# A searched table takes the place of a rehearsed schedule, and the clamp of the norm moves to VectorE

## The chip, the core and the metric

The kernel runs on one core of one Trainium2 chip. The metric is the device time of one execution in microseconds (us). The engines have short names in the profile: PE is TensorE (PEld its weight loads), DVE is VectorE, ACT is ScalarE, POOL is GpSimd, SP is the engine that issues most DMAs. [...]

## The reference

An attention block with inducing points feeds a SwiGLU feed-forward block. There are B = 4 batches of N = 12416 rows of C = 128 numbers, m = 32 inducing rows, and a hidden width of 1536.

```python
def mab(q, kv):
    s = scale * (q @ kv.transpose(0, 2, 1))
    s = s - s.max(-1, keepdims=True)
    a = np.exp(s)
    a /= a.sum(-1, keepdims=True) + 1e-09
    return a @ kv
h = mab(I, x)                 # 32 inducing rows look at all rows of the batch
x = mab(x, h)                 # every row looks at the 32 results
...
rms = np.sqrt(np.mean(x * x, axis=-1, keepdims=True) + 1e-06)
xn = x / rms * rms_g
g = xn @ w_gate
silu = g * (1.0 / (1.0 + np.exp(-g)))
val = xn @ w_val
return silu * val @ w_out
```

All is float32. The second attention's weights have only 32 numbers a row, so the kernel never forms the attention's output: it multiplies h into the gate and value weights once for each batch (the stacks `sg` and `sv`) and applies them to the 32 weights of each row. The norm needs only a 32 x 32 matrix of products of h (`gram`) and those weights. The clamp of the diff stands in that norm: the mean square is held at 1e-6 or more before the power -1/2.

## The kernel before, in words

**Slots.** A batch is cut into 7 sets of rows, and these into 25 units: 20 of 512 columns, 4 of 480 and one of 256. A unit has 12 slots, one for each block of 128 hidden numbers. There are 300 slots for each batch and 1200 in all. A slot is written by `slot` in `ffn`: the gate product (L723, one pass of PE into a PSUM bank `gv`), SiLU on ScalarE (L731; in a few slots tanh at L727 with two more VectorE operations), the value product (L734), their product on VectorE (L740), and then the steps of other work that are due.

**Three kinds of block.** The output product of a block (`u` times a block of `w_out`) can be done in two ways.
- A plain block writes the product to a buffer `u` in SBUF, and PE takes it in float32 at L660 (two records each in the trace, `acc<-u,wo`).
- A three-pass block is split into parts of fewer bits, and PE takes three faster passes: L681 and L683 into the bank `u3`, L660 into `acc` (`project3`). The kind "sums" leaves the product in its PSUM bank (L740, `gv<-silu,gv`), takes the high part on ScalarE (L705), the rest on VectorE (L706) and the difference of both on POOL (L715). The kind "differences" writes `u`, and needs two ScalarE copies (L709, L714) and two POOL operations (L710, L715). The parts lie in rings of buffers (`idle` holds the free ones).

A string of letters gives each slot its kind: `s`, `d`, or `.` for plain. The strings before have three parts of 300; the second serves batches 1 and 2.

**Order of products.** Products are not done in the slot that makes their operand, but some slots later, first in, first out in two lists (`plain` and `kara`). Before the gate product a slot calls `products(0)`, before the value product `products(1)`, and before the n-th step of other work `products(n + 2)`. What each call does is in `picks`. Before the change, `rehearse` fills `picks`: a model in Python with fixed costs for each step (`COST`) that walks through all slots as the engines would, and whenever PE would stand idle takes a product that is ready, or up to two when more than a reserve of seven are waiting.

**Banks and buffers.** The products of gate and value and most attention steps share five PSUM banks `gv0` to `gv4`. The rehearsal also gives the banks: always the one that comes free first. `u` has nine buffers, `work` three, both taken in turn.

**Other work in the slots.** While the slots of batch b run, the first attention of batch b + 1 is done in steps that `schedule(b)` puts at fixed slots: `turn_x` (VectorE transposes of loaded columns), `scores1`, `max1` to `max3`, `exp1_of`, `turn_e`, `sum_h`, `fold_l`, `divide`, `turn_h`, `square_h`, `stack`, `place` (DMAs that put pieces of the new stacks in place), `scores2`, `row_max`, `sub_max`, `exp2`. For each set of rows there is a seam, which scales its attention weights by the norm: `turn_a`, `square` (L507), `turn_z` (L513, L514), `scale` (L518), `root` (two POOL operations, L523 the clamp and L524 the power), `apply` (L528), `turn_b` (L532), `split` (L538, L541). Then `gather`, a DMA of the split halves, brings each unit's operand `a` ten slots before the unit starts. The loop at the end of the kernel calls, in each slot, the steps that are due now (`waiting`), then those of the plan. After the last slot all remaining products are done, plain ones first, and then what is still in `waiting`.

Of the kernel before, what the change touches and what calls it, by code (L numbers as in the profile page):

```python
# [18 lines left out]
P = 128  # L19
R = 4  # L20
# [3 lines left out]
def kernel(  # L24
# [87 lines left out]
    work = pool("work", 3)  # L112
# [4 lines left out]
    up = pool("up", HELD)  # L117
# [46 lines left out]
    nc.gpsimd.memset(mhalf[:], -0.5)  # L164

# [9 lines left out]
    sel = up.tile([P, 512], F32R, name="u")[:, 0:2 * P].rearrange("p (k r c) -> p k r c", k=2, r=R)  # L175
# [39 lines left out]
    def rounding(i, c):  # L215
# [20 lines left out]
        def power():  # L236
# [12 lines left out]
            e = st["e"] = work.tile([P, 512], I32, name="we", tag="work")  # L249
# [38 lines left out]
    BANKS5, turn, turns = 5, [0], []  # L288

    def bank():  # L290
        if turns:
            n = turns.pop(0)
        else:
            n = turn[0] % BANKS5
            turn[0] += 1
        return ps_gv.tile([P, 512], F32, name="gv", tag=f"gv{n}")

    def attention(b, load_next):
# [42 lines left out]
        def max2():  # L341
            ps = bank()
            nc.tensor.transpose(ps[0:1, 0:P], st["mx"][:], ident[:])
            row = once.tile([1, m], F32, name="row")
            nc.vector.reduce_max(out=row[:], in_=ps[0:1, 0:P].rearrange("p (q m) -> p m q", m=m), axis=AX.X)
            row4 = st["row4"] = once.tile([1, R, m], F32, name="row4")
            nc.vector.tensor_scalar_mul(out=row4[:], in0=row[:].unsqueeze(1).to_broadcast((1, R, m)), scalar1=-SCALE)

        def max3():
            ps = bank()  # L350
            nc.tensor.matmul(ps[:, 0:1], st["row4"][:].rearrange("p q m -> p (q m)"), ones[0:1, 0:1],
                             start=True, stop=True)
            nbias = st["nbias"] = small.tile([P, 1], F32, name="nbias")
            nc.vector.tensor_copy(out=nbias, in_=ps[:, 0:1])

        def exp1_of(s0, s1):
# [8 lines left out]
            if s1 == NS:  # L365
                nc.vector.reduce_sum(out=st["hl"][:, C:C + 1], in_=st["ls"][:, 0:k + 1], axis=AX.X)

        def turn_e(s):
            e = st["e", s] = (once.tile([P, P], F32, name="hT") if b and per[s] < R else
                              work.tile([P, per[s] * m], F32, name="e", tag="work") if b else  # L370
                              up.tile([P, 512], F32, name="u"))[:, 0:per[s] * m]
# [20 lines left out]
        def fold_l():  # L392

            ps = bank()
# [61 lines left out]
        def stack(i):  # L456
# [5 lines left out]
            hi, lo = st["halves", i] = [work.tile([P, 512], F32R, name=n, tag="work") for n in ("whi", "wlo")]  # L462
# [28 lines left out]
    def seam(b, s):  # L491
# [9 lines left out]
        def turn_a():  # L501
            eT = st["eT"] = work.tile([P, 512], F32, name="eT", tag="work")
# [6 lines left out]
        def turn_z():  # L509
            ps = st["ps"]  # L510
            z = st["z"] = work.tile([P, n, m], F32, name="z", tag="work")
# [4 lines left out]
        def scale():  # L516
            ms = numbers("ms")
            nc.vector.reduce_sum(out=ms, in_=st["z"][rows, :, :], axis=AX.X)  # L518
            st["ms"] = ms

        def root():
            rs = st["rs"] = numbers("rs")
            nc.gpsimd.tensor_scalar(out=rs, in0=st["ms"], scalar1=1e-6, scalar2=None, op0=ALU.max)  # L523
            nc.gpsimd.tensor_tensor(out=rs, in0=rs, in1=mhalf[rows, 0:n], op=ALU.pow)  # L524
# [5 lines left out]
        def turn_b():  # L530
            aT = st["aT"] = work.tile([P, 512], F32, name="aT", tag="work")
# [38 lines left out]
    def soon(k, step):  # L570

        waiting.append([k, step])

# [73 lines left out]
    def ffn(b, u):  # L647
# [72 lines left out]
        def slot(j, products, steps, tanh):  # L720
# [14 lines left out]
            t = v if kinds.get((b, u, j)) == "sums" else up.tile([P, 512], F32, name="u")  # L735
# [109 lines left out]
    if B > 1:  # L845
        for _ in range(R):
            load_channels(*pieces[1].pop(0))

    COST = {"turn_x": (0, .63), "scores1": (1.07, .7), "max1": (0, .1), "max2": (.23, .85), "max3": (.2, .1), "turn_e": (0, .63),
            "exp1_of": (0, 0, 1.14), "sum_h": (2.0, .25), "fold_l": (.16, .15), "divide": (0, .6), "turn_h": (.3, .8),  # L850
            "square_h": (.2, .76), "stack": (1.3, 1.32), "scores2": (1.19, .63), "row_max": (0, .59), "sub_max": (0, 0, 0, 1.01),
            "exp2": (0, 0, 1.0), "turn_a": (0, .63), "square": (1.02,), "turn_z": (0, 1.23), "scale": (0, .6),
            "root": (0, 0, 0, 2.9), "apply": (0, 0, 0, 1.01), "turn_b": (0, .63), "split": (0, 0, .51, 1.25),
            "power": (0, .45), "power_number": (0, 0, .63), "upper": (0, .6), "upper_number": (0, 0, .53), "sign": (0, .6),
            "lower": (0, .6, 0, 1.26), "stack_of": (.87, 0, .5), "stack_low": (0, .62), "split_wo": (0, 0, .7, 1.52), "split_last": (0, 0, .35, .65)}
    BANKS = {"scores1", "sum_h", "max2", "max3", "fold_l", "turn_h", "square_h", "stack", "scores2", "square", "stack_of"}
    AFTER = {"max2": "max1", "max3": "max2", "fold_l": "exp1_of", "turn_h": "divide", "square_h": "turn_h", "square": "turn_a",
             "sum_h": "turn_e", "scores1": "turn_x", "stack": "turn_h", "root": "scale", "apply": "root"}
    ENGINES = ("PE", "DVE", "ACT", "POOL")
    TAIL = {"PE": .17, "DVE": .09, "ACT": .11, "POOL": .04}  # L860
# [96 lines left out]
    def near(b, k, first, last):  # L957
        return any(e + first <= k < e + last for e in plans[b][1])

    def given(b, k, u, j):  # L960
        return plans[b][0].get(k, []) + seams.get((b, u, j), [])

    kinds, picks = {}, {}
    letters = """
        ..........................dd...dsd...d....dssd..dssdss.ssd..sdd.sdd.dd...ss.ssd.ss...dsdsdd.s...sssd
        sdd..s..sdsssd.dsd..dsdd..dd.s......s..ddd..dssssssssd..dssssd.ssd..s.d.ssssss..ssssssssdd..ss.dddss
        sd..dsssssd.ss..s.sdss.sds..ssssssssds..s.ssdssd.d..s...d.d..s..s.s.sdsssd...ss.ss.s.s..ssdssssddd..
        ..ssdd..sd..sd.ssdds.d...sds.s.s.s...dssdsd.sd..dsssd.ss.d..ssdssdd.s...ssdd..sdsd...ssssddsds...sss
        .ssdsd..sds.sds.dd..dsssd..d.d.....ss.ds.d..sssssdsssd..sdsssdss.s..sdds.ss.ss..ssssssdsdd...sdssssd
        sd..d.sssdds.s..ssss.ssssd..s.ssssdssd..ssss.sdssd.....sd.d.....s.sssd.s.s...sssd.ssss..ssssssssds..  # L970
        .s....dss..ssdsssd.sss..sd..s.d.sssss.sssds..sdssssss.s.ss.sssdsssd...s.sss..sd.sssss.sss.dsdssdss.s
        ss.ss.sssss.sds.ssd..ss.sds..sd.ssssd..ssssss..ssds.sssss.ssssd..s.ssss..sds.sssssssssd..ssssssss.ds
        ..sssssss.dsds.s..ssss.ds.sssdds...ssss.ssssssdsss..sdsssd...s..sss.s..dsssdd.ds...dsssssssd.sd.dd..
    """
    letters = "".join(letters.split())
    BLOCKS = [letters[NU * NJ * n:NU * NJ * (n + 1)] for n in (0, 1, 1, 2)]

    def rehearse():

        at = dict.fromkeys(ENGINES, 0.0)  # L980
        free, open_banks = [0.0] * 5, {}
        taken, done = [0.0] * SILU, {}
        rounded = {weight[one]["lower"]: one for one in chunks}
        queues, uses, later, left = {"plain": [], "three": []}, [0], [], {}
        split = {"u3": 0.0, "all": 0}
        idle, leaving = list(range(RING)), []

        def run(e, us, *after):
            at[e] = max([at[e]] + [one + 0.04 for one in after]) + us
            return at[e] + TAIL[e]  # L990

        def bank():
            n = free.index(min(free))
            turns.append((n + turn[0]) % BANKS5)
            return n

        def soon(k, step):
            later.append([k, step])

        def bank_of(unit):  # L1000
            older = flat.index(unit) - 2
            if older < 0 or flat[older] not in left:
                return 0.0
            return left[flat[older]].get("turned", 1e9)

        def has(kind, by):
            if not queues[kind]:
                return False
            t, unit = queues[kind][0][:2]
            if left[unit]["left"] == NJ:  # L1010
                t = max(t, bank_of(unit))
            if kind == "three" and not left[unit]["three"]:
                t = max(t, split["u3"])
            return t <= by

        def ready():
            return sum(one[0] <= at["PE"] for q in queues.values() for one in q)

        def issue(kind, to):
            to.append(kind)  # L1020
            t, unit, w, n = queues[kind].pop(0)
            split["all"] -= 1
            st = left[unit]
            if st["left"] == NJ:
                t = max(t, bank_of(unit))
                assert t < 1e9
            if kind == "plain":
                end = run("PE", 0.858 * w, t)
            else:
                end = run("PE", 0.697 * w, t)  # L1030
                give_back(n, idle, leaving)
                st["three"] += 1
                st["open"] -= 1
                st["end"] = end
                copy(st, w)
            st["left"] -= 1
            st["end"] = end
# [200 lines left out]
```

## Time and profile before

| | us |
|---|---|
| median of 3 runs (lowest, highest) | 1615.83 (1615.65, 1616.07) |
| the profiled execution | 1615.95 |
| its span, first to last instruction | 1614.0 |
| PE matmul busy | 1593.5 (99%) |
| DVE busy | 1438.5 (89%) |
| POOL busy | 1434.7 (89%) |
| ACT busy | 1307.4 (81%) |
| PE weight loads busy | 1100.1 (68%) |

The first slot's gate product starts at 54.5 us; the batches' first gate products are at 54.5, 461.1, 852.5 and 1245.2 us. DMA takes a small share (70 GB/s on average). In the groups of the page each line gives source line, engine, operation, tiles, shapes, count, then busy time and the mean length of one in ns, then the idle time of the engine just before and who ended it. In a timeline the columns are the start, the length, the engine, the line and the operation, and in brackets the idle time before it with what ended it. Matmuls overlap, so that the step from one start to the next tells what one costs.

### The profile page before, as it was taken

Reading aid. Unit: us, or ns where it says so; the run is one execution under the profiler, and the core shown is the slowest. Engines: PE = TensorE matmul, PEld = TensorE weight load, DVE = VectorE, ACT = ScalarE, POOL = GpSimd, SP = SyncE. Lnnn points to the kernel's source line nnn. Section 1 sums busy time; section 2 is a strip of 40 time slices with the busy share of each in tenths; the row PEclk is TensorE's granted clock in tenths of the full one; section 3 lists DMA queues with packets and bytes.
Section 4 is the critical chain, followed back from the end, with each engine's and each line's share of the span. In section 5 each row is a group of like instructions: output and inputs, shape, how many; then the busy total and the mean of one; then the engine's idle time right before and its main releaser. Section 6 shows DMA issues by size and latency. Waiting matters only on the chain.

```text
span 1614.0 us, 26024 instructions
## 1 busy us (share of the span) xinstructions
PE 1593.5 (99%) x7169; PEld 1100.1 (68%) x7169; DVE 1438.5 (89%) x2471; ACT 1307.4 (81%) x2461; POOL 1434.7 (89%) x1182
## 2 busy tenths in 40 slices
PE   8999999999999999999999999999999999999998
PEld 6546667756676666776677666676667677777776
DVE  4879988999889997999888999799989999999996
ACT  4678888877887888887888888888788888888886
POOL 1379999999899999999888999899988899999997
PEclk9999999999999999999999999999999999999999
DMA  7455524443462241624344323262221212212111
GB/s 263 92 74 85 104 52 89 94 97 60 72 97 50 44 95 27 134 64 96 65 68 79 62 42 82 49 139 69 57 38 30 39 30 40 40 27 44 36 37 28
DMA packets 389186, 112.57 MB, mean 70 GB/s; under 512 B 365072, under 2 KB 369712, under 8 KB 386480
## 3 DMA queue, kind: packets, MB, share of 16 engines
q1 hardware_dynamic: 388304, 110.82, 34.9%
q8 instruction: 57, 0.93, 0.3%
q14 instruction: 89, 0.73, 0.2%
q10 hardware_dynamic: 736, 0.08, 0.0%
HBM read 53.95 MB, written 27.00 MB: 50 GB/s over the span
## 4 chain that ended last, share of the span: by engine, by line
PE 83%; POOL 5%; ACT 3%; issue 2%; DVE 1%; SPq 1%; DMA 0%; POOLq 0%; DVEq 0%; ACTq 0%
PE acc L660 28%; PE gv L723 16%; PE gv L734 15%; PE u L683 10%; PE u L681 10%; PE gv L330 2%; POOL xn L715 2%; POOL rs L524 1%; PE gv L386 1%; POOL xn L710 1%; PE gv L507 1%; ACT silu L731 1%; SPq L470 0%; ACT sc L447 0%; ACT xn L705 0%
## 5 line engine op out<-in xcount | busy, mean ns | idle before, releaser
L731 ACT ACTIVATE silu<-gv 128x512 f32<-128x512 f32 (+2 forms) x1186 | 688.8, 587 | 166.0 <-PE gv L723 150.2
L715 POOL TENSOR_TENSOR xn<-xn,xn 128x512 fp32r<-128x512 f32 (+2 forms) x605 | 745.7, 1252 | 70.2 <-DVE xn L706 30.2
L734 PE MATMUL gv<-a,sv 128*128 128x512 f32 (+2 forms) x1188 | 603.3, 508 | 1.3 <-DVE u L740 0.6
L723 PE MATMUL gv<-a,sg 128*128 128x512 f32 (+2 forms) x1188 | 486.3, 410 | 4.6 <-ACT silu L731 2.2
L740 DVE TENSOR_TENSOR u<-silu,gv 128x512 f32<-128x512 f32 (+2 forms) x633 | 414.9, 661 | 68.6 <-PE gv L734 35.5
L660 PE MATMUL acc<-u,wo 128*128 128x512 f32 (+2 forms) x822 | 410.7, 583 | 0.6 <-DVE u L740 0.6
L740 DVE TENSOR_TENSOR gv<-silu,gv 128x512 f32<-128x512 f32 (+2 forms) x553 | 367.7, 668 | 44.1 <-PE gv L734 31.5
L723 PEld LDWEIGHTS gv<-a,sg 128*128 128x128 f32 x1188 | 223.8, 188 | 171.8 <-ACT silu L731 37.2
L734 PEld LDWEIGHTS gv<-a,sv 128*128 128x128 f32 x1188 | 223.8, 188 | 123.4 <-issue 43.1
L705 ACT ACTIVATE xn<-gv 128x512 fp32r<-128x512 f32 (+2 forms) x434 | 253.1, 583 | 58.6 <-DVE gv L740 47.4
L706 DVE SCALAR_TENSOR_TENSOR xn<-xn,gv 128x512 fp32r<-128x512 f32 (+2 forms) x434 | 284.5, 655 | 10.5 <-ACT xn L705 5.8
L681 PE MATMUL u<-xn,xn 128*128 128x512 f32 (+2 forms) x581 | 228.5, 393 | 0.0
L660 PE MATMUL acc<-xn,more 128*128 128x512 f32 (+2 forms) x581 | 226.4, 390 | 1.9 <-POOL xn L715 1.9
L710 POOL TENSOR_TENSOR xn<-u,xn 128x512 fp32r<-128x512 f32 (+2 forms) x171 | 216.1, 1264 | 13.3 <-ACT xn L709 13.3
L660 PEld LDWEIGHTS acc<-u,wo 128*128 128x128 f32 x822 | 154.1, 188 | 36.9 <-issue 5.1
L660 PEld LDWEIGHTS acc<-xn,more 128*128 128x128 f32 x581 | 109.0, 188 | 32.1 <-POOL xn L715 10.3
L681 PEld LDWEIGHTS u<-xn,xn 128*128 128x128 f32 x581 | 109.2, 188 | 25.7 <-issue 5.3
L715 POOL TENSOR_TENSOR sg<-sg 128x512 fp32r<-128x512 f32 (+1 forms) x92 | 118.1, 1283 | 5.5 <-DVE sg L706 1.7
L715 POOL TENSOR_TENSOR sv<-sv 128x512 fp32r<-128x512 f32 (+2 forms) x92 | 118.0, 1282 | 5.4 <-DVE sv L706 2.8
L709 ACT ACTIVATE xn<-u 128x512 fp32r<-128x512 f32 (+2 forms) x171 | 105.5, 617 | 17.6 <-DVE u L740 14.4
L683 PE MATMUL u<-xn,more 128*128 128x512 f32 (+2 forms) x294 | 113.3, 385 | 0.2 <-POOL xn L710 0.2
L683 PE MATMUL u<-xn,xn 128*128 128x512 f32 (+2 forms) x287 | 110.3, 384 | 0.0
(202 smaller groups left out, 1918.4 us busy)
## 6 DMA issues: line engine op xcount, KB each, us to landing
out_dram<-o SPq DMA_DIRECT2D x320, 64.0 KB, 2.0
xT<-in_x_dram SPq DMA_DIRECT2D x60, 256.0 KB, 5.0
xn<-in_x_dram SPq DMA_DIRECT2D x60, 256.0 KB, 5.3
a<-hi SPq DMA_DIRECT2D x156, 64.0 KB, 2.0
a<-lo SPq DMA_DIRECT2D x156, 64.0 KB, 2.0
xn<-in_x_dram SPq DMA_DIRECT2D x5, 1024.0 KB, 10.0
xn<-w SPq DMA_DIRECT2D x18, 256.0 KB, 3.4
out_dram<-o SPq DMA_DIRECT2D x64, 60.0 KB, 1.9
```

Of the source, the lines that this page charges most:

```text
L660: nc.tensor.matmul(acc[:, 0:T], lhsT, rhs, start=st["left"] == NJ, stop=st["left"] == 1)
L681: nc.tensor.matmul(ups[:, 0:T], weight_of(0, j), hi, start=st["k"] == nk, stop=False)
L683: nc.tensor.matmul(ups[:, 0:T], weight_of(1, j), lo, start=False, stop=not st["k"])
L705: nc.scalar.activation(hi, v, AF.Copy, scale=(1.0 - 2.0 ** -13) * 2.0 ** -12)
L706: nc.vector.scalar_tensor_tensor(out=lo, in0=hi.bitcast(F32), scalar=-4096.0, in1=v, op0=ALU.mult, op1=ALU.add)
L709: nc.scalar.activation(d, v, AF.Copy, scale=1.0 - 2.0 ** -13)
L710: nc.gpsimd.tensor_tensor(out=lo, in0=v, in1=d.bitcast(F32), op=ALU.subtract)
L715: nc.gpsimd.tensor_tensor(out=d, in0=hi.bitcast(F32), in1=lo.bitcast(F32), op=ALU.subtract)
L723: nc.tensor.matmul(g[:, 0:T], sg[:, ts(j, P)], a[:, 0:T], start=True, stop=True)
L731: nc.scalar.activation(sl[:, 0:T], g[:, 0:T], AF.Silu)
L734: nc.tensor.matmul(v[:, 0:T], sv[:, ts(j, P)], a[:, 0:T], start=True, stop=True)
L740: nc.vector.tensor_tensor(out=t[:, 0:T], in0=sl[:, 0:T], in1=v[:, 0:T], op=ALU.mult)
```

## The change

The model `rehearse`, its costs and its tables are gone. In their place stand tables, found by a search, for the kind of each block (now four parts, one for each batch), the slot of each listed step (`places`; steps keep their kinds and arguments, and are sorted by slot), the products before each gate and value product and step (`ordered`: groups are divided by commas, slots by semicolons, `p` is plain and `t` three-pass), the PSUM bank of each use (`banks`), and the buffer of each `work` tile and of each `u` (`workers`, `holders`). The number of buffers stays: five banks, three `work`, nine `u`.

The clamp moves: the sum of squares is written beside a constant 1e-6 in pairs (`least`), and VectorE takes the maximum over each pair; POOL's `root` is one operation instead of two. A small sum (`reduce_sum` of `ls`) moves from the last `exp1_of` to `fold_l`, and `row4` shares a buffer with `hg`. The steps before the first slot are otherwise as they were.

```diff
-    work = pool("work", 3)
+    work = pool("work", 1)
...
-    up = pool("up", HELD)
+    up = pool("up", 1)
...
+    least = const.tile([P, 16, 2], F32, name="least")
+    nc.gpsimd.memset(least[:], 1e-6)
...
+    def worker(shape, dtype, name):
+        return work.tile(shape, dtype, name=name, tag=f"work{works.pop(0)}")
...
         def scale():
             ms = numbers("ms")
-            nc.vector.reduce_sum(out=ms, in_=st["z"][rows, :, :], axis=AX.X)
+            nc.vector.reduce_sum(out=least[rows, 0:n, 0], in_=st["z"][rows, :, :], axis=AX.X)
+            nc.vector.reduce_max(out=ms, in_=least[rows, 0:n, :], axis=AX.X)
             st["ms"] = ms
...
             rs = st["rs"] = numbers("rs")
-            nc.gpsimd.tensor_scalar(out=rs, in0=st["ms"], scalar1=1e-6, scalar2=None, op0=ALU.max)
-            nc.gpsimd.tensor_tensor(out=rs, in0=rs, in1=mhalf[rows, 0:n], op=ALU.pow)
+            nc.gpsimd.tensor_tensor(out=rs, in0=st["ms"], in1=mhalf[rows, 0:n], op=ALU.pow)
...
-            t = v if kinds.get((b, u, j)) == "sums" else up.tile([P, 512], F32, name="u")
+            t = v if kinds.get((b, u, j)) == "sums" else up.tile([P, 512], F32, name="u", tag=f"u{factors.pop(0)}")
...
+    def placed(b):
+
+        steps = [(k, *one) for k, (u, j) in slots(b) for one in given(b, k, u, j)]
+        moved = sorted(zip([int(k) for k in places[b].split()], range(len(steps))))
+        at = {}
+        for k, n in moved:
+            at.setdefault(k, []).append(steps[n][1:])
+        return at
...
-    rehearsed = rehearse()
+    kinds = {(b, u, j): marks[letter] for b in range(B) for (k, (u, j)), letter in zip(slots(b), "".join(letters[b].split()))
+             if letter in marks}
+    picks = [line.split(",") for line in "".join(ordered.split()).split(";")]
+    turns += [(int(c) + turn[0]) % NB for c in "".join(banks.split())]
+    works += [int(c) for c in "".join(workers.split())]
+    factors += [int(c) for c in "".join(holders.split())]
...
-                for n, (step, args) in enumerate(given(b, k, u, j)):
+                wait()
+                for n, (step, args) in enumerate(at.get(k, [])):
                     products(n + 2)
                     step(*args)
...
-    while kara or plain:
-        (plain.pop(0) if plain else kara.pop(0))()
-    while waiting:
-        waiting.pop(0)[1]()
+    while kara or plain or waiting:
+        wait()
+        give(picks.pop(0)[0] if picks else "")
```

The tables begin like this (the order of products of the first slots, and a stretch further on in batch 0):

```python
    ordered = """
        ;;;,p;,pp;;,pp;;,pp;;,pp;;;,pp,,,p;;,p;;;,p;;;p;,p;;,p;;,p;;;,pp;,pp;,pp;,tt;;,tp,t;;,p;;,tp;;,tp;;,pp;;,tt;,t;
...
        ,t;,p;;,t;,tt;;,p;,tt;,tp;;,tp;,t;;;,tt;,pt;;,t;;t,t;;p,t;;;t,t;,p;t;,tp;;,tt;,p;;,tp;,t;;,tp;;,p;,tt;;t;,tp;;
```

## The prediction

> **What bounds the kernel now.** I read the page's head first, then busy time by stage (one window for each batch, cut at its first gate product), then the waits, then PE's timeline, start to start. The head of the page:
>
> ```profile
> span 1614.0 us, 26024 instructions
> ...
> PE 1593.5 (99%) x7169; PEld 1100.1 (68%) x7169; DVE 1438.5 (89%) x2471; ACT 1307.4 (81%) x2461; POOL 1434.7 (89%) x1182
> ...
> PE   8999999999999999999999999999999999999998
> ...
> DVE  4879988999889997999888999799989999999996
> ...
> POOL 1379999999899999999888999899988899999997
> ```
>
> PE is full from start to end, and VectorE (DVE) and GpSimd (POOL) run at 89% behind it: three engines with little room. The windows (columns: stretch, length, busy time and instructions of each engine, granted clock, DMA share, GB/s) are batches 0 to 3, the last cut at 1600, and the end:
>
> ```profile
> 54.50:461.10 406.60, 401.92 (x1745) 263.00 (x1746) 360.86 (x615) 325.90 (x605) 352.69 (x288) 1.00 0.46 83
> 461.10:852.50 391.40, 390.00 (x1736) 266.52 (x1734) 353.75 (x609) 322.23 (x610) 363.72 (x298) 1.00 0.39 74
> 852.50:1245.20 392.70, 390.33 (x1733) 266.40 (x1733) 354.45 (x609) 322.44 (x607) 361.92 (x295) 1.00 0.32 64
> 1245.20:1600.00 354.80, 354.74 (x1401) 260.12 (x1400) 332.35 (x550) 305.50 (x576) 338.10 (x275) 1.00 0.19 36
> 1600.00:1614.00 14.00, 8.06 (x48) 6.48 (x46) 5.31 (x13) 5.54 (x18) 8.48 (x12) 0.94 0.18 28
> ```
>
> PE's visible idle time is 4.7 us in batch 0, 1.4 and 2.4 in the next two, nothing in the last, 5.9 in the final 14 us. So the time is PE's work, plus stalls of a few tens of us at most. Matmul ends are modelled and hide short stalls. I therefore took each PE start against the usual spacing of the same neighbours: the excess comes to about 21 us between 130 and 1600 us, spread over all batches in pieces of 0.1 to 0.6 us.
>
> PE's prices are read from starts. A three-pass block takes 102.72 to 103.42, 0.70 us. A plain block and the value product behind it take 103.42 to 104.52, 1.10 us; a single pass is 0.23, so the plain block costs 0.87.
>
> ```profile
> 102.72 0.40 PE L681 MATMUL u<-xn,xn 128*128 128x512 f32 x1
> 102.96 0.39 PE L683 MATMUL u<-xn,xn 128*128 128x512 f32 x1
> 103.19 0.40 PE L660 MATMUL acc<-xn,more 128*128 128x512 f32 x1
> 103.42 1.02 PE L660 MATMUL acc<-u,wo 128*128 128x512 f32 x2
> 103.88 0.80 PE L734 MATMUL gv<-xn,sv 128*128 128x512 f32 x1
> 104.52 0.40 PE L723 MATMUL gv<-xn,sg 128*128 128x512 f32 x1
> ```
>
> The largest single stall is batch 0's first seam. POOL's power (L524) and scaling (L528) come late, VectorE's turn (L532) stands in its queue and waits 2.45 us, the product behind it (L740) is late, and the gate product finds no free bank for 2.08 us:
>
> ```profile
> 114.19 2.94 POOL L524 TENSOR_TENSOR rs<-rs,mhalf 128x16 f32<-128x16 f32 x1
> 116.76 0.79 PE L734 MATMUL gv<-a,sv 128*128 128x512 f32 x1
> 117.21 1.05 POOL L528 TENSOR_TENSOR sc<-sc,rs 128x512 f32<-128x512 f32 x1
> 118.29 0.71 DVE L532 STREAM_TRANSPOSE aT<-sc 128x512 f32<-128x512 f32 x1 [2.45 <-POOL sc L528]
> 118.92 0.65 DVE L740 TENSOR_TENSOR u<-silu,gv 128x512 f32<-128x512 f32 x1
> 119.63 0.50 PE L723 MATMUL gv<-a,sg 128*128 128x512 f32 x1 [2.08 <-DVE u L740]
> ```
>
> ```profile
> 116.00:124.00 8.00, 5.92 (x14) 3.00 (x13) 5.48 (x9) 5.05 (x10) 7.74 (x7) 0.79 0.09 20
> ```
>
> The granted clock of that window is 0.79: the stall costs 2.1 us idle and some 1.7 us (0.21 of 8) of slow clock.
>
> [...] 354.74 of 354.80 us are busy in the last batch, while starts still show small excesses. [...] Here 2.1 us of visible idle time were followed by slow passes (gate product to gate product 121.49 to 124.03, 2.54 us against 1.33 for the same three products)[...]. [...]
>
> **The change part by part.** The sum is made against the profiled execution: 1615.95 us, of which the span is 1614.0; the median of the runs is 1615.83, 0.1 us below it.
>
> *Kinds of blocks.* Counted in the letters: sums 561 to 593, differences 228 to 218, plain 411 to 389. So 22 blocks become three-pass: 19 more of 512 columns, 11 more of 480, 8 fewer of 256. At 512 each saves 0.87 - 0.70 = 0.17. At 480 the timeline near 405 us gives 0.80 - 0.66 = 0.14; at 256, near 1602, about 0.45 - 0.35 = 0.10. PE: 19 x 0.17 + 11 x 0.14 - 8 x 0.10 = **-4.0 us**, on the path. It is paid beside PE: VectorE 32 more L706 at 0.66, +21 us; ScalarE (ACT) 32 more L705 at 0.58, 10 fewer each of L709 and L714 at 0.62, +6; POOL 22 more L715 at 1.25, 10 fewer L710 at 1.26, +15. With the clamp below, VectorE reaches 1464 and POOL 1442 of some 1603 us, 91% and 90%. Cover is PE's work; the thinnest place is the last batch, where VectorE goes from 337.7 to about 342 of some 366 us.
>
> *Clamp.* 28 POOL operations (L523, 0.26 us) go, -7.4 us on POOL. 28 VectorE maxima over 16 pairs come. No such row exists: the nearest, maxima over 7 numbers (L339), take 0.15; [...] a reduction of 512 elements (L518) takes 0.63. I take 0.15, +4 us on VectorE, hidden beside PE; at 0.63 it would be 18 us, and VectorE 92% busy. The chain to the power shortens by 0.1 us. Off the path: 0, from -1 to +2 us.
>
> *First seam.* Its power moves from slot 36 to 35 and its scaling to 37; the turn stays at 39. One slot is about 1.2 us, and POOL's 0.26 goes: the scaling comes 1.4 us earlier of the 2.45 that the turn waited. The first scores also come two slots earlier. Of 2.1 + 1.7 us I count **-2.7**; from 0 to -3.8.
>
> *Attention, seams, queues.* 416 of the 659 listed steps move, at most ten slots; loads, fetches, sum_h and exponentials stay. In a seam the power moves 1.6 slots forward on average and the scaling 1.9 back, which lets other POOL work between two operations that together hold the queue for 3.7 us; the split comes 3 slots later, at most 6, while its first reader is a gather that is issued ten slots ahead of the gate product that needs it. On SP only the stack pieces move (at most ten slots later, some 80 slots before they are read); gathers and loads stand behind them, with the same ten slots in hand. Each moved step costs what it cost: 0. Two waits may come late: the last sub_max of a batch now stands at slot 250 to 253, ahead of the exponential at 256 (it was 246), 3 to 6 slots or some 4 to 8 us for a 1 us operation in a POOL queue 92% full; and work tiles taken again one or two slots after the piece that empties them, which already costs VectorE 1.7 us once (L513 on the DMA from whi, in the groups). Up to +1 us a batch.
>
> *Order of products.* In the order of the two built programs, weighted by the PE prices above, a three-pass block now has longer between its value product and its first pass: sums 6.3 to 6.9 us in the median, the lowest hundredth 3.2 to 3.9. POOL's late results were the 0.5 to 0.6 us stalls near 497, 623, 889 and 1016 us; those should go. Plain blocks come sooner, 8.3 to 6.9, still far above VectorE's 0.66. Against it, products now go in pairs, with bare slots between: bare slots 62 to 337, and a gate bank is written again within 1.4 us in 256 cases instead of 99. In the trace of before such writes came 0.01 to 0.06 us late: 157 x 0.02 = +3 us. Of the 21 us of small stalls I let a third go: -7 + 3 = **-4 us**, from -14 to +10.
>
> *End.* After the last value product (1604.68) five products ran until 1609.1, with waits of 0.38, 0.18, 0.18 and 0.42: 4.4 us for 1.95 us of work. After it come three plain and one three-pass block, about 1.7 us, without the last POOL result: **-2.2 us**, from 0 to -2.7.
>
> Sum: -4.0 - 2.7 - 4 - 2.2 = -12.9; 1615.95 - 12.9 = **1603 us**.
>
> **Rivals.** (a) Only the work counts: new stalls eat what the order saves. 1615.95 - 4.0, about 1612; for it speaks that three engines run above 90%. (b) Slower: bare slots run out of gv banks. Gate, value, gate, value follow in 0.93 us, while ScalarE alone needs 0.59 for each SiLU and 0.58 for each split, so the fifth write waits for a bank. Each of 275 more bare slots would pay 0.07 us, +19 us, less 4.0 + 2.7 + 2.2: about 1626. It decides from (8.9 + 3.2) / 275 = 0.044 us a slot. Against it: the 62 bare slots of before show 0.02. (c) The searched order removes most small stalls: -14 instead of -4, 1593. (d) It doesn't do what it says, e.g. the tile names bring a wait on a buffer that turned freely before: there are nine u and three work buffers on both sides, so this would look like (b), smaller; I count it there.
>
> **How the numbers follow.** Forecast 0.50, (c) 0.12, (a) 0.22, (b) with (d) 0.16. Within 0.2% (1612.6 to 1619.1, about what a measurement of this kernel can tell from no change) falls half of (a). Faster 0.50 + 0.12 + 0.11 = 0.73, same 0.11, slower 0.16. The range leaves out most of (b) and the far end of (c): 1593 to 1618.
>
> **What would show it.** Right: PE's last batch shorter by 1 to 4 us with PE still full; L706 x593 groups in sum; window 116 to 124 with a clock above 0.9; no POOL-released stall of 0.5 us on L660; the end under 12 us. Wrong: PE idle before L723 or L734 released by ScalarE or VectorE, adding up to over 10 us; or VectorE's maxima at 0.6 us.

## The result, and the profile after

The median fell from 1615.74 to 1594.82 us (lowest 1592.14, highest 1597.52), a ratio of 0.9871 with an interval of 0.9851 to 0.9891: faster by 20.9 us. The forecast was 1603, with 1593 to 1618 around it. The sign and the order of size were right; two terms of the sum, the clamp and the order of products, were too small, and the term of the first seam rested on a wrong cause. The middle of the forecast is 8 us off, and the median lies 1.8 us inside the lower end of its range.

The four runs of the kernel after lie 5.4 us apart (two near 1592.6 us at a mean granted clock of 1.000, the profiled one among them, and two near 1597 at 0.998 and 0.999), those of the kernel before 1.1 us, and why is open. The profiled execution took 1593.12 us, against 1615.95 before. The head of its page and the shares of the chain that ended last (followed back from the last instruction, at each step to what released it):

```profile
span 1591.2 us, 26159 instructions
...
PE 1577.6 (99%) x7191; PEld 1108.7 (70%) x7191; DVE 1458.6 (92%) x2531; ACT 1300.7 (82%) x2473; POOL 1442.6 (91%) x1167
...
PE 94%; DVE 1%; DMA 0%; issue 0%; POOL 0%; ACT 0%; SPq 0%; POOLq 0%; DVEq 0%; ACTq 0%
```

The same last line of the page of the kernel before:

```profile
PE 83%; POOL 5%; ACT 3%; issue 2%; DVE 1%; SPq 1%; DMA 0%; POOLq 0%; DVEq 0%; ACTq 0%
```

VectorE and GpSimd are fuller than before, and yet they have nearly left the chain. It ran through POOL for 5% and ACT for 3% of the span; now both round to nothing. The windows of the kernel after (stretch, length, busy time and instructions of each engine, granted clock, DMA share, GB/s) are the four batches, the last 14 us, and the place of the old first stall:

```profile
55.40:452.70 397.30, 396.46 (x1751) 264.40 (x1751) 365.27 (x633) 321.76 (x604) 349.24 (x280) 1.00 0.47 85
452.70:839.50 386.80, 386.14 (x1739) 268.75 (x1738) 360.53 (x624) 323.33 (x616) 365.69 (x294) 1.00 0.39 75
839.50:1225.50 386.00, 385.47 (x1744) 269.77 (x1744) 360.96 (x627) 320.92 (x612) 368.31 (x296) 1.00 0.33 66
1225.50:1577.20 351.70, 351.01 (x1395) 259.04 (x1394) 333.32 (x557) 303.05 (x578) 342.12 (x273) 1.00 0.19 36
1577.20:1591.20 14.00, 9.10 (x56) 8.05 (x54) 6.57 (x16) 5.86 (x17) 7.62 (x10) 0.99 0.17 27
116.00:124.00 8.00, 7.85 (x30) 5.26 (x28) 7.98 (x15) 7.28 (x14) 7.92 (x8) 1.00 0.14 34
```

Batches 0 to 2 are 9.3, 4.6 and 6.7 us shorter, and the last, with the end, 3.1. Counted as in the prediction (each PE start against the usual spacing of the same neighbours), PE's stalls fell from 30.1 to 11.5 us over the whole span: 21.3 to 10.1 between 130 and 1600 us, 5.8 to 1.3 between 60 and 130, 1.3 to 0.1 before that, 1.7 to nothing at the end. These 18.6 us and the 4.0 us of work that the kinds save are 22.6 of the 22.8 us between the two profiled executions. The count is good to a few us only: in kinds_only below it grows by 43.5 us where the length and the saved work allow 38.4, in places_only by 31.2 for 27.7 us of length.

A finer measure takes the time apart by stretches: the start of the first gate product, of the gate products of slots 60 and 1140, and the end, each taken from the trace. Where an edit touches nothing, two profiled executions agree within 0.1 us in the stretches behind the start-up (tail_kinds against before; no such pair exists for the kernel after); the start-up itself varies by up to 1 us, and is longer in the two root_longer kernels, since batch 0's first root stands in it. The numbers are the length of each stretch minus its length before; a product deferred across a cut moves a little time between neighbouring stretches.

| profiled execution | start-up | slots 0-59 | 60-1139 | 1140 to the end | sum |
|---|---|---|---|---|---|
| after | +0.9 | -3.4 | -17.9 | -2.4 | -22.8 |
| kinds_only | +0.2 | +0.3 | +34.9 | -1.1 | +34.4 |
| clamp_only | 0.0 | -1.9 | -3.9 | -0.1 | -5.9 |
| places_only | +0.4 | -1.1 | +27.9 | +0.5 | +27.7 |
| clamp_back | +1.0 | -2.4 | -15.8 | -2.0 | -19.3 |
| rehearsed_all | +0.1 | +2.3 | +12.2 | -0.8 | +13.7 |
| unpaired | +0.1 | -4.1 | -13.7 | -2.5 | -20.2 |
| buffers_in_turn | +0.2 | -3.3 | -17.1 | -2.4 | -22.7 |
| first_seam | +1.0 | -1.2 | -0.7 | -0.1 | -0.9 |
| root_longer_before | +2.2 | +1.0 | +10.7 | 0.0 | +13.9 |
| root_longer_after | +2.0 | -2.2 | -11.6 | -1.9 | -13.7 |
| kinds_back | +0.6 | -3.4 | -14.0 | -2.4 | -19.2 |
| tail_kinds | 0.0 | 0.0 | 0.0 | -1.1 | -1.2 |

### The profile page after: what moved, and what is told of

It reads as the page before. It is cut to its first block, busy times and chain, and to the rows that moved or that the text cites. A ratio compares the mean times of both kernels' runs of the same rounds, so it can differ in the third digit from the quotient of the medians.

```text
span 1591.2 us, 26159 instructions
## 1 busy us (share of the span) xinstructions
PE 1577.6 (99%) x7191; PEld 1108.7 (70%) x7191; DVE 1458.6 (92%) x2531; ACT 1300.7 (82%) x2473; POOL 1442.6 (91%) x1167
## 4 chain that ended last, share of the span: by engine, by line
PE 94%; DVE 1%; DMA 0%; issue 0%; POOL 0%; ACT 0%; SPq 0%; POOLq 0%; DVEq 0%; ACTq 0%
PE acc L679 31%; PE gv L742 18%; PE gv L753 17%; PE u L702 11%; PE u L700 11%; PE gv L336 3%; PE gv L512 1%; PE gv L390 1%; DMA a<-lo 0%; PE gv L466 0%; PE gv L480 0%; DVE u L759 0%; POOL lo L546 0%; SPq L558 0%; DVE gv L759 0%
## 5 line engine op out<-in xcount | busy, mean ns | idle before, releaser
L734 POOL TENSOR_TENSOR xn<-xn,xn 128x512 fp32r<-128x512 f32 (+2 forms) x620 | 767.1, 1257 | 46.1 <-DVE xn L725 20.2
L753 PE MATMUL gv<-a,sv 128*128 128x512 f32 (+2 forms) x1188 | 569.1, 480 | 0.7 <-DVE u L759 0.4
L742 PE MATMUL gv<-a,sg 128*128 128x512 f32 (+2 forms) x1188 | 483.8, 408 | 1.8 <-DMA a<-lo 1.3
L759 DVE TENSOR_TENSOR u<-silu,gv 128x512 f32<-128x512 f32 (+2 forms) x595 | 387.1, 655 | 46.7 <-PE gv L753 22.3
L759 DVE TENSOR_TENSOR gv<-silu,gv 128x512 f32<-128x512 f32 (+2 forms) x591 | 395.9, 674 | 35.5 <-PE gv L753 17.9
L679 PE MATMUL acc<-u,wo 128*128 128x512 f32 (+2 forms) x778 | 379.8, 577 | 0.0
L742 PEld LDWEIGHTS gv<-a,sg 128*128 128x128 f32 x1188 | 223.4, 188 | 150.9 <-issue 33.1
L724 ACT ACTIVATE xn<-gv 128x512 fp32r<-128x512 f32 (+2 forms) x460 | 271.0, 589 | 54.1 <-DVE gv L759 38.4
L725 DVE SCALAR_TENSOR_TENSOR xn<-xn,gv 128x512 fp32r<-128x512 f32 (+2 forms) x460 | 304.0, 661 | 6.9 <-ACT xn L724 4.0
L700 PE MATMUL u<-xn,xn 128*128 128x512 f32 (+2 forms) x599 | 243.9, 407 | 0.0
L729 POOL TENSOR_TENSOR xn<-u,xn 128x512 fp32r<-128x512 f32 (+2 forms) x160 | 199.0, 1244 | 8.1 <-ACT xn L728 8.1
L734 POOL TENSOR_TENSOR sv<-sv 128x512 fp32r<-128x512 f32 (+1 forms) x95 | 122.6, 1291 | 5.4 <-PE acc L679 1.0
L702 PE MATMUL u<-xn,xn 128*128 128x512 f32 (+2 forms) x290 | 111.6, 385 | 0.0
L728 ACT ACTIVATE xn<-u 128x512 fp32r<-128x512 f32 (+2 forms) x160 | 98.1, 613 | 15.3 <-DVE u L759 10.7
## 6 DMA issues: line engine op xcount, KB each, us to landing
xn<-in_x_dram SPq DMA_DIRECT2D x5, 1024.0 KB, 10.2
```

Of the source, the lines that this page charges most:

```text
L679: nc.tensor.matmul(acc[:, 0:T], lhsT, rhs, start=st["left"] == NJ, stop=st["left"] == 1)
L700: nc.tensor.matmul(ups[:, 0:T], weight_of(0, j), hi, start=st["k"] == nk, stop=False)
L702: nc.tensor.matmul(ups[:, 0:T], weight_of(1, j), lo, start=False, stop=not st["k"])
L724: nc.scalar.activation(hi, v, AF.Copy, scale=(1.0 - 2.0 ** -13) * 2.0 ** -12)
L725: nc.vector.scalar_tensor_tensor(out=lo, in0=hi.bitcast(F32), scalar=-4096.0, in1=v, op0=ALU.mult, op1=ALU.add)
L728: nc.scalar.activation(d, v, AF.Copy, scale=1.0 - 2.0 ** -13)
```

## The experiments

Times are medians; ratios are to the kernel before, run beside each on the same chip (1615.1 to 1616.0 us).

### One part at a time: kinds, clamp, slots

**kinds_only** puts the new letters into the kernel before, which rehearses its order and banks for them. The new strings begin like this:

```diff
+    letters = [
+        """
+        ..........................dss.sdd...ss.sd.dsss..s.dss.dsds..sdsdsd...s..dsdd.sd..s..sd..sdsssd..ss.d
...
+    BLOCKS = ["".join(one.split()) for one in letters]
```

> The kernel before with the new letters alone (four strings, 22 more three-pass blocks); the rehearsal plans products, banks and slots as before. If the gain is PE work plus a better order of products (theory A), this shows the work: 3 to 5 us faster than before, about 1612. If the new kinds themselves fit the other engines better and so remove the stalls (theory B), it shows at least half of the 21 us: 1605 or less. If the 32 more VectorE rests and 22 more GpSimd differences hurt without the new order, it is not faster than 1615.

Measured: 1650.44 us, ratio 1.0216 (1.0202 to 1.023). The kinds that save 4 us of PE's work make the kernel 34.5 us longer where the old rehearsal orders the products: stalls rose from 30.1 to 73.6 us, spread over all batches. The end alone gained, 1.1 us.

**clamp_only** moves only the clamp (and lets `row4` share its buffer, as after).

```diff
-            nc.vector.reduce_sum(out=ms, in_=st["z"][rows, :, :], axis=AX.X)
+            nc.vector.reduce_sum(out=least[rows, 0:n, 0], in_=st["z"][rows, :, :], axis=AX.X)
+            nc.vector.reduce_max(out=ms, in_=least[rows, 0:n, :], axis=AX.X)
...
-            nc.gpsimd.tensor_scalar(out=rs, in0=st["ms"], scalar1=1e-6, scalar2=None, op0=ALU.max)
-            nc.gpsimd.tensor_tensor(out=rs, in0=rs, in1=mhalf[rows, 0:n], op=ALU.pow)
+            nc.gpsimd.tensor_tensor(out=rs, in0=st["ms"], in1=mhalf[rows, 0:n], op=ALU.pow)
```

> The kernel before with the clamp as a maximum over pairs on VectorE (and row4 in the buffer of hg, to have room for the pairs); all else as before, with the rehearsal's old costs. Theory A: hidden beside PE, within 1 us of before (1615 to 1617), except that the first seam's 2.45 us wait gets 0.1 us shorter. If GpSimd's queue is what delays PE (theory C), 7 us less on GpSimd brings 2 to 5 us.

Measured: 1610.13 us, ratio 0.9965 (0.9953 to 0.9978), faster by 5.9. It was forecast at nothing. A seam of batch 1 in the timeline of the kernel before shows what the forecast missed:

```profile
493.59 0.25 POOL L523 TENSOR_SCALAR rs<-ms 128x16 f32<-128x16 f32 x1
493.92 2.93 POOL L524 TENSOR_TENSOR rs<-rs,mhalf 128x16 f32<-128x16 f32 x1
496.82 1.29 POOL L715 TENSOR_TENSOR xn<-xn,xn 128x512 fp32r<-128x512 f32 x1
498.16 0.50 PE L660 MATMUL acc<-xn,more 128*128 128x512 f32 x1 [0.28 <-POOL xn L715]
```

The clamp and the power hold POOL's queue for 3.23 us, from 493.59 to 496.82. The difference L715 of a three-pass block stands behind them, and PE's last pass of that block waits for it. The same place in clamp_only:

```profile
490.45 2.90 POOL L526 TENSOR_TENSOR rs<-ms,mhalf 128x16 f32<-128x16 f32 x1
493.31 1.29 POOL L717 TENSOR_TENSOR xn<-xn,xn 128x512 fp32r<-128x512 f32 x1
```

The queue is held 2.86 us. The clamp took 0.37 us of it, more than its own 0.25, and POOL's hold over all 28 roots (from the first operation of the root to the start of the next on POOL) fell from 89.3 to 79.1 us. So POOL was not off the path. More POOL work, below, tests that its time is what counts, and not the buffer that `row4` now shares. It lengthens the chain to the power along with the queue; that PE waits for what stands behind the power in the queue is read from the waits and from the chain of before, and no run holds the queue without the chain to the power.

**places_only** moves only the listed steps, through the same `placed` as the kernel after.

```diff
-                for n, (step, args) in enumerate(given(b, k, u, j)):
+                for n, (step, args) in enumerate(moved_to[b].get(k, [])):
```

> The kernel before with the listed steps at the new slots; kinds, clamp and the rehearsal as before. Theory A (order of products and banks): only the first seam's stall gets smaller, 2 to 4 us faster, about 1612. Theory C (the slots of attention and seams hold up GpSimd and VectorE less, and that is what removes the small stalls): 8 us or more, 1607 or less. A loss would say that the slots only fit the new order.

Measured: 1642.85 us, ratio 1.0168 (1.0154 to 1.0182), slower by 26.9; the stalls came to 61.3 us. One row of its waits (waiting engine, tile and line, releaser, us in total, times, longest) shows one kind of loss:

```profile
DVE aT L532 <- POOL sc L528: 15.0, 9, 3.5
```

VectorE's turn stands nine times in front of its queue for POOL's scaling, 15.0 us in all; in the kernel before three such waits came to 3.1 us. The moved steps find POOL later than they were placed for. How much of the 26.9 us comes through this wait is not shown.

### The parts together, the tables apart

**clamp_back** is the kernel after with the clamp on POOL again (the two lines of clamp_only's diff, the other way round). PE's order of instructions is that of the kernel after.

> The changed kernel with the clamp back on GpSimd (two operations in root, one reduction on VectorE), tables unchanged. Theory A: 0 to 1 us slower than the changed kernel's 1594.8, since VectorE and GpSimd both have cover. If the searched order needs the shorter GpSimd queue (theory C), 3 us or more slower, 1598 or more.

Measured: 1596.53 us, ratio 0.9879 (0.9865 to 0.9892). It is 1.7 us slower than the kernel after by the medians, with intervals that overlap, and 3.5 by the table of the profiled executions. The tables carry most of the gain; the clamp is worth less with them than without.

**rehearsed_all** keeps the new kinds, slots and clamp, and gives the order of products and the banks back to the old rehearsal, with a reserve of six in place of seven, and lets the buffers turn.

```diff
-    RING, RESERVE, HELD, SILU = 4, 7, 9, 3
+    RING, RESERVE, HELD, SILU = 4, 6, 9, 3
```

> All of the change but the tables of products, banks and buffers: new kinds, new slots of the steps and the clamp on VectorE, with the products and banks of the old rehearsal (its reserve at six waiting blocks instead of seven, since with seven it finds no order). Theory A (the order of products and banks is what takes the stalls away): 1630 us or more, like the two parts alone (1650 and 1643), so that the tables are worth 35 us or more on top of the same work. Theory D (kinds and slots fit each other, and only one of them alone hurts): 1612 or less.

Measured: 1629.58 us, ratio 1.0086 (1.0071 to 1.0101), with 47.2 us of stalls. The same work with the tables takes 34.8 us less. The model was not fitted anew to this plan, so this is the difference between these two orders, not between a search and any rehearsal.

POOL is the smaller part of what is lost here: the weight loads of last passes wait 4.6 us for the difference of an `xn` block, and 0.4 in the kernel after. The larger rows are those of gate and value products, which take a bank again after SiLU has read it. In rehearsed_all:

```profile
PEld gv L725 <- ACT silu L733: 43.0, 128, 0.9
PEld gv L736 <- ACT silu L733: 25.3, 66, 1.3
```

After:

```profile
PEld gv L742 <- ACT silu L750: 23.4, 75, 1.0
PEld gv L753 <- ACT silu L750: 15.7, 58, 0.7
```

Only a part of these 68.3 and 39.1 us of waiting weight loads is lost to PE: its own visible idle time until SiLU, before the same products, is 7.8 and 0.7 us. Whether the order or the choice of banks makes these waits is not shown.

**unpaired** takes 187 pairs of products apart: the second goes into the next slot that had none.

```diff
-        ;;;,p;,pp;;,pp;;,pp;;,pp;;;,pp,,,p;;,p;;;,p;;;p;,p;;,p;;,p;;;,pp;,pp;,pp;,tt;,tp,t;;,p;;,tp;;,tp;;,pp;;,tt;,t;
+        ;;;,p;,p;,p;,p;,p;,p;,p;,p;,p;;,pp,,,p;;,p;;;,p;;;p;,p;;,p;;,p;;;,pp;,pp;,pp;,tt;,tp,t;;,p;;,t;,p;,t;,p;,p;,p;
```

> The changed kernel with 187 of its pairs of products taken apart: where a slot takes two products before its value product and the next slot takes none, the second goes into that next slot. Kinds, slots, banks and buffers as in the changed kernel. If pairs with bare slots are what helps (theory E), the gain is mostly lost: 1606 or more. If pairs are only how the search happened to place them, and the length from value product to first pass counts (it gets longer for the 187), the time stays within 3 us of 1594.8.

Measured: 1595.70 us, ratio 0.988 (0.9866 to 0.9895): the kernel after within the intervals (0.9 us more by the medians, 2.6 by the profiled executions). The pairs are not the gain. Nor do they cost what rival (b) feared: with fewer bare slots, 178 in place of 337 in the trace, the kernel is not faster.

**buffers_in_turn** lets `u` and `work` turn as before, nine and three in one ring each; the order of products and the banks stay those of the tables.

```diff
-            t = v if kinds.get((b, u, j)) == "sums" else up.tile([P, 512], F32, name="u", tag=f"u{factors.pop(0)}")
+            t = v if kinds.get((b, u, j)) == "sums" else up.tile([P, 512], F32, name="u", tag="u")
```

> The changed kernel with its nine u and three work buffers taken in turn, as before the change, instead of by the table. Theory A: 0 to 2 us slower than 1594.8, the tables of buffers only follow the order. If a wait on a buffer is what the tables remove (theory F), 5 us or more slower.

Measured: 1593.06 us, ratio 0.9862 (0.9848 to 0.9877). The tables of buffers bring nothing. So the 34.8 us lie in the order of products and the choice of banks. A version with the banks in plain turn was not run, and how the gain divides between those two is open.

### The first seam

**first_seam** is the kernel before with the sum of squares and the power of batch 0's first seam one slot earlier and its scaling one later, about as the table has them.

```diff
-                j = ((14, 17, 18, 21, 22, 23, 29, 31) if k else (32, 33, 34, 35, 36, 36, 39, 41))[i]
+                j = ((14, 17, 18, 21, 22, 23, 29, 31) if k else (32, 33, 34, 34, 35, 37, 39, 41))[i]
```

> The kernel before with one edit: in the first seam, scale and root come one slot earlier (34 and 35) and apply one later (37), as in the changed kernel; the rehearsal plans around it. Theory A: the 2.1 us stall at 116.8 us and the slow clock behind it (1.7 us) go for the larger part: 2.5 to 4 us faster than before, 1612 to 1613.5. If the turn on VectorE then waits as long as before, no change.

Measured: 1614.67 us, ratio 0.9995 (0.9987 to 1.0004), unresolved; slots 0 to 59 are 1.2 us shorter. VectorE's turn in its timeline:

```profile
119.55 0.71 DVE L532 STREAM_TRANSPOSE aT<-sc 128x512 f32<-128x512 f32 x1 [2.28 <-POOL sc L528]
```

It still waits 2.28 us, before 2.45. Naming earlier slots did not bring the power forward. Against the first gate product (54.48 and 55.45) the sum of squares starts 57.47 us in, before 57.63, and the power 60.01, before 59.71. VectorE comes to the sum of squares at 112.92, when L514 ahead of it (0.71 us from 112.17) is done, and POOL to the clamp and the power when L715, L710 and L715, ahead of them in both kernels, are done: the last of these runs 1.30 us from 112.47 before, and 1.29 us from 113.74 here, and the clamp starts at 113.86 and 115.12. The gate product's stall fell from 2.08 to 1.7 us.

### How much POOL's time costs, before and after

**root_longer_before** adds two more maxima on POOL to each root of the kernel before, and nothing else.

```diff
+            nc.gpsimd.tensor_scalar(out=rs, in0=rs, scalar1=1e-6, scalar2=None, op0=ALU.max)
+            nc.gpsimd.tensor_scalar(out=rs, in0=rs, scalar1=1e-6, scalar2=None, op0=ALU.max)
```

> The kernel before with two more maxima against 1e-6 on GpSimd in each root (0.26 us each, 0.53 us a seam, 15 us of GpSimd over the kernel); the order of all other instructions is untouched. Taking 0.26 us a seam away (clamp_only) brought 5.7 us. Theory A (PE waits for GpSimd behind each power, because the old order leaves three-pass blocks too little time): 0.53 us a seam costs 8 us or more, 1624 or more. If the gain of clamp_only was something else, such as the shared row buffer, 1619 or less.

Measured: 1629.12 us, ratio 1.0082 (1.0064 to 1.01): 14.1 us for 18.3 us more of POOL's queue (107.6 against 89.3). The order of PE's instructions is that of the kernel before, so nothing but POOL's time changed.

**root_longer_after** adds two maxima to each root of the kernel after in the same way.

> The changed kernel with the same two extra maxima on GpSimd in each root, 15 us of GpSimd. Theory A (the new order gives three-pass blocks more time, so that PE no longer waits behind a power): clearly less than in the kernel before, 1 to 5 us, 1596 to 1600. If GpSimd at 91% simply has no room left, as much as in the kernel before or more: 1603 or more.

Measured: 1601.68 us, ratio 0.9912 (0.9894 to 0.993): 6.9 us more than the kernel after, for 19.1 us of POOL's queue (98.8 against 79.7). That lies between the two expectations. By the profiled executions it is 9.1 us, against 13.9 before. POOL is not free there either, but an added microsecond costs about half to two thirds of what it did (0.36 to 0.48 us against 0.77).

The waits view shows the wait itself. The rows are those of the weight load of a three-pass block's last pass, which waits for POOL's difference (us in total, times, longest). Before:

```profile
PEld acc L660 <- POOL xn L715: 10.5, 30, 0.9
```

clamp_only and root_longer_before, the same instructions under shifted line numbers:

```profile
PEld acc L662 <- POOL xn L717: 3.2, 10, 0.6
```

```profile
PEld acc L662 <- POOL xn L717: 20.9, 46, 1.5
```

After, clamp_back and root_longer_after:

```profile
PEld acc L679 <- POOL xn L734: 0.4, 1, 0.4
```

```profile
PEld acc L679 <- POOL xn L734: 2.6, 10, 0.4
```

```profile
PEld acc L681 <- POOL xn L736: 8.4, 23, 0.9
```

With one order of PE the wait runs 3.2, 10.5, 20.9 us as POOL's hold grows 79, 89, 108 us. With the other it runs 0.4, 2.6, 8.4 for 80, 90, 99. The second order leaves three-pass blocks more time before their last pass, and what POOL is late by is mostly covered. The traces show this time: the differences on POOL and the last passes come in the same order, so each can be paired with its own. The last pass starts within 0.2 us of the end of its difference in 43 of 789 blocks before (18 in clamp_only, 63 in root_longer_before), and in 2 of 811 after (16 in clamp_back, 35 in root_longer_after). The median time between the two is 1.18 us before and 1.64 after.

### Kinds and the end

**kinds_back** is buffers_in_turn with 36 of the sums blocks of 512 columns plain again, each product at the same place in the order.

```diff
-        ..........................dss.sdd...ss.sd.dsss..s.dss.dsds..sdsdsd...s..dsdd.sd..s..sd..sdsssd..ss.d
+        ..........................dss..dd...ss.sd.ds.s..s.dss.dsds..sdsdsd......dsdd.sd..s..sd..sdss.d..ss.d
```

> The changed kernel (buffers in turn, which made no difference) with 36 of its sums blocks of 512 columns made plain, spread over the kernel; each such product stays at its place in the order. PE's work grows by 36 x 0.17 = 6.1 us, VectorE loses 36 rests and GpSimd 36 differences. If PE's work counts in full: 1599 (593 to 595 plus 6). If VectorE's and GpSimd's relief pays for it: 1596 or less. If the order suffers: 1602 or more.

Measured: 1596.71 us, ratio 0.989 (0.9873 to 0.9906), 3.7 us above buffers_in_turn, single runs up to 1601.5; the profiled spans differ by 3.5 (1594.8 and 1591.3). At the prediction's 0.17 us a block the work alone is 6.1. The slot lengths, in the account of the kinds below, give 5.8 us of work and 2.6 us of stalls that went, which leaves 3.2; the count of starts sees only 0.9 of them (12.2 to 11.3).

**tail_kinds** gives the last unit of the kernel before the twelve letters that it has after.

```diff
+    BLOCKS[3] = BLOCKS[3][:-NJ] + "s.ssd....d.."
```

> The kernel before with the kinds of the last unit's twelve blocks as in the changed kernel (differences and sums early, plain blocks last). Theory A: only the end changes, fewer three-pass blocks are left when the last value product is done: 1.5 to 2.5 us faster, 1613 to 1614.3. If the end is set by the output's transpose and DMA alone: no change.

Measured: 1614.84 us, ratio 0.9996 (0.9988 to 1.0005): the medians don't resolve it. In the profiled execution the last stretch is 1.1 us shorter and every other within 0.1, and kinds_only shows the same 1.1 there. So the letters are some half of the end's 2.4.

## Why the prediction was right, and where it was wrong

**What bounds the kernel** held: PE's work and small stalls in PE's stream, to be read from starts. Most of the gain came from those stalls, which the page's 99% hides on both sides.

**Kinds, -4.0: right as work.** The counts are there (593 sums). So is the price, when the length of every slot in both traces, from one gate product to the next, is fitted as a sum over what the slot holds (least absolute deviations; either trace alone gives the same within 0.01 us): a plain block takes 0.86 us and a three-pass block 0.70 at 512 columns, 0.80 and 0.65 at 480, 0.43 and 0.36 at 256. With these the 22 blocks save 4.1 us. But the cover named, PE's work beside fuller VectorE and POOL, is not given by the kinds themselves: without the tables they cost 34.5 us.

**Clamp, 0 within -1 to +2: wrong when taken alone.** The instruction on VectorE was priced well: it is 0.19 us long, and the next one starts 0.10 later (109.83 to 109.93 below); the 0.15 taken from the maxima over 7 numbers lies between. The step that failed is "off the path": POOL's 7.4 us were taken to be hidden beside PE. They were 10.2 us of queue (0.37 instead of 0.26 each) ahead of differences that PE waited for, and removing them gave 5.9 us. The trace of before already had this. The chain that ended last, listed piece by piece, holds six of the 28 powers at full length:

```profile
114.19 2.94 POOL rs L524
228.62 2.93 POOL rs L524
493.92 2.93 POOL rs L524
620.07 2.93 POOL rs L524
885.13 2.93 POOL rs L524
1012.64 2.93 POOL rs L524
```

The clamp of each stands in the chain too, just ahead of its power, and in five of the six the next piece is a difference (L715) that stood behind the power in the queue, not the scaling. In clamp_only one power is left in that chain, in root_longer_before there are ten (a difference follows nine of them), in the kernel after none. Some 1.9 of the 5.9 us lie in the first 60 slots, where the first seam's stall shrank to 1.4 us. The prediction had seen those waits near 497 us, and credited them to the order alone. In the kernel after both remove the same wait, so the clamp's own share there is small (1.7 to 3.5 us, not resolved) and the two gains don't add.

**First seam, -2.7: a fair size by luck, for a wrong reason.** Slots 0 to 59 are 3.4 us shorter, and the slow clock is gone: the window from 116 to 124 shows 1.00 instead of 0.79. But first_seam shows that the earlier slot alone is not the cause. In the timeline of the kernel after:

```profile
109.83 0.19 DVE L524 TENSOR_REDUCE ms<-least 128x16 f32<-128x32 f32 x1
109.93 0.68 DVE L759 TENSOR_TENSOR u<-silu,gv 128x512 f32<-128x512 f32 x1
110.75 2.90 POOL L529 TENSOR_TENSOR rs<-ms,mhalf 128x16 f32<-128x16 f32 x1
113.73 1.05 POOL L533 TENSOR_TENSOR sc<-sc,rs 128x512 f32<-128x512 f32 x1
114.81 0.71 DVE L537 STREAM_TRANSPOSE aT<-sc 128x512 f32<-128x512 f32 x1
```

The whole chain stands earlier: the sum of squares starts at 109.12 (before 112.11) and the power at 110.75 (before 114.19), although the first gate product is 0.9 us later. Up to slot 34 PE has done 25 plain and 4 three-pass products where it had done 28 and 2, so it reaches the seam's slots sooner (the gate product of slot 34 starts at 106.59 instead of 108.02). VectorE then does eight other operations between the maximum and the turn, and the turn waits for nothing. The working counted slots; it should have asked when VectorE and POOL get to them. Kinds, order and places act together here, and no run divides them.

**Attention, seams, queues, 0.** No run gives the old slots to the kernel after, so their share with the tables is not known. Under the old order of products the same moves cost 26.9 us. The statement "each moved step costs what it cost" can hold only for a plan whose other parts fit, not for the moves as such. One small cost is seen: the gather behind the split, taken to have ten slots in hand, now holds PE up twice, 1.3 us in all (`DMA a<-lo` in the row of L742 below); before, no gate product waited for it.

**Order of products, -4: the term that was mis-sized.** Its mechanism was right: the longer lead of three-pass blocks did away with the POOL-released stalls (10.5 to 0.4 us in the rows above; 2.6 with the clamp still on POOL). "A third go" was too little: 11.2 of 21.3 us went. The 3 us of new bank waits were not seen; the gate and value products of the kernel after, as groups of its page (busy time, mean ns, then idle time and what ended most of it):

```profile
L753 PE MATMUL gv<-a,sv 128*128 128x512 f32 (+2 forms) x1188 | 569.1, 480 | 0.7 <-DVE u L759 0.4
L742 PE MATMUL gv<-a,sg 128*128 128x512 f32 (+2 forms) x1188 | 483.8, 408 | 1.8 <-DMA a<-lo 1.3
```

PE stood 2.5 us before all of them, 1.3 for an operand and 1.1 for a bank; before the change it was 5.9. Their weight loads, too, waited less for SiLU and the product, 78.2 us in place of 88.7, although those of the value products waited more (28.0 in place of 20.4). So the 3 us don't appear. That refutes rival (b) at its place, with its 337 bare slots present. Rival (d) falls with buffers_in_turn. Rival (c), 1593, is nearest to the measured time; its term of -14 is nearer to the order's -11.2 than the -4 chosen. Rival (a) undercounts by 17 us.

**End, -2.2.** From the last value product to the end it took 9.33 us before and takes 6.80. In the timeline of the kernel after:

```profile
1584.38 0.28 PE L753 MATMUL gv<-a,sv 128*128 128x256 f32 x1
1584.49 1.02 PE L679 MATMUL acc<-u,wo 128*128 128x256 f32 x4
1585.17 0.47 PE L700 MATMUL u<-sg,xn 128*128 128x256 f32 x1
...
1585.71 0.59 PE L679 MATMUL acc<-u,wo 128*128 128x256 f32 x2
```

PE issues its last block 1.33 us after the last value product; before, the last product started 4.17 us after it (1604.68 to 1608.85). The step stands: 2.5 us against 2.2.

## What to carry to other kernels

When several engines run near 90% behind a full one, price the queue ahead of each consumer, not the engine's share: 0.37 us on POOL ahead of a late operand cost PE more than half of it, and the same 0.37 us cost a third or less once the consumer stood later. Here the chain that ended last, of the kernel before, had shown this queue. Kinds, places and order of such a plan are one setting: new kinds alone cost 34.5 us and new slots alone 26.9 under a rehearsal that was not fitted to them, while all of it together gained 20.9, so a part tried by itself tells little of its worth in the whole. Adding work to one engine under both orders (a dose) shows how much of it is covered in each.

## What the runs showed of the hardware that was not expected

- A maximum on POOL of 0.25 us, ahead of the power that needs it, holds the queue for longer: 0.37 us by taking 28 of them away, 0.33 to 0.34 by adding 56. Busy time misses the rest.
- PE's clock fell after some of the stalls and not after others. Visible idle times of 1.4 us (clamp_only), 1.7 us (first_seam) and 1.8 us (places_only) kept 1.00 in the windows from 116 to 124; 2.1 us (before) was followed by 0.57 between 120 and 124 us, and 2.8 us (root_longer_before) by 0.76 between 124 and 130. But in rehearsed_all 1.6 us, at 127.6, was followed by 0.78 between 127.9 and 135.5, so the length of the gap alone doesn't tell.
